# One group of transposes moved from TensorE to DMA, small loads to ScalarE's queue, and a rewritten order of work in a gated long-convolution and MLP kernel

## The chip, the core and the metric

The kernel runs on one core of a Trainium2 chip. A core has TensorE (PE in the profile; it multiplies, and it also transposes 128x128 blocks by multiplying with an identity), VectorE (DVE), ScalarE (ACT), GpSimd (POOL) and SyncE (SP, which here issues nearly all DMAs). ScalarE can issue DMAs too. TensorE writes only to PSUM, and VectorE or ScalarE must move each result from there to SBUF: such a move is called an evacuation below. The metric is the device time of one execution in microseconds (us).

## The reference

The inputs are q, k, v of 2048 tokens by 512 channels, a short kernel `shift_k` of 4 taps per channel, a long kernel `ssm_k` of 2048 taps per channel, a skip weight `ssm_D`, and an MLP of width 1376. The output is four residual layers on x = q:

```python
def _A_ref(q, k, v, shift_k, ssm_k, ssm_D):
    # k_shift[s] = sum over t of k[s - 3 + t] * shift_k[:, 3 - t]
    kv = k_shift * v
    y = irfft(rfft(pad(kv)) * rfft(pad(ssm_k)))[:S]      # causal convolution along the tokens
    y = y + kv * ssm_D
    return q * y
def _B_ref(x, w1, b1, w2, b2):
    y = _layernorm(x, axis=-1)
    return gelu(y @ w1 + b1) @ w2 + b2

x = A_q
x = x + _A_ref(_layernorm(x), A_k, A_v, A_shift_k, A_ssm_k, A_ssm_D)
x = x + _B_ref(_layernorm(x), B_w1, B_b1, B_w2, B_b2)
x = x + _A_ref(_layernorm(x), A_k, A_v, A_shift_k, A_ssm_k, A_ssm_D)
x = x + _B_ref(_layernorm(x), B_w1, B_b1, B_w2, B_b2)
```

The convolution does not depend on x, so it is computed once and its result y is used by both A layers.

## The kernel before, in words

The work has two parts. The first, up to about 100 us, computes y. The second runs the two MLP layers over the 16 token tiles in groups of four, eight rounds in all, each of two matrix products with the next group's normalisation beside them. The second part is not touched.

The first part consists of small pieces, each with a name. `plan.add` gives a piece its cost, what it depends on, and which buffer rings it takes from; `mm_evac` makes two pieces at once, a TensorE piece and its evacuation, whose name ends in `e`. The costs in the code are those that an offline planner used; at run time they have no effect. What the planner found is the long string `ORDER`: one word for each piece, such as `K26e.A` or `X01.20`. The letter after the dot is the engine (P TensorE, D VectorE, A ScalarE, G GpSimd, S SyncE); digits are buffer numbers, for a TensorE piece that of the PSUM buffer it fills. The kernel is written out in that order, so every engine runs its own pieces strictly in that order, and a piece that waits holds up all that stand behind it on its engine. There are four PSUM buffers `p` of 1024 float32 columns; a TensorE piece must wait until the one named for it is evacuated.

The pieces, in about the order of the data (cc counts four groups of 128 channels, j four groups of eight frequencies):

- loads: `lk0` to `lk3` (k), `lh1`, `lh113` (k, shifted rows), `lv0`, `lv1` (v), `lK00` to `lK11` (the long kernel, 128-byte runs), `lX`, `lW`, `lM` (transform tables), `lx0`, `lx1` (q, token groups 0 and 1), `lx` (all of q as the residual x), `lsT` and `lSK` (the short kernel, twice), `w1` to `w4` (MLP weights and output bias), `lb0`, `lb1` (the first MLP bias, loaded as single 2-byte elements).
- `kT`: transposes of k. `dg`: diagonal matrices of the short kernel. `kv`: the short convolution of channel groups 0 to 2 on TensorE, and `kvm` its product with v on VectorE. Group 3 has its short convolution on GpSimd: `kg0`, `kg1`, `ka1`, ..., `ka3`, then `kgm`, the product with v. Its two scratch tiles are T buffers 0 and 2, which the `T` pieces take later.
- `s00`, `s10`: layer-norm statistics of token groups 0 and 1, either on VectorE (batch-norm instructions) or on ScalarE (eight passes); `s01`, `s11`: what GpSimd adds to them; `s02`: the normalisation of group 0.
- `U`: the forward transform of kv, first stage (`U1S0` and so on), then a transposition: on TensorE (`U1T0`, `U1T1`, sixteen 128x128 blocks each, with an evacuation of 2048 columns) or by a DMA with transpose. `UT = "PPPX"` says which, one letter for each channel group: P TensorE, X DMA.
- `kd`, `KS`, `K2`: the transform of the long kernel; `sa0` to `sb3`: copies of it from SBUF to SBUF with its rows exchanged.
- `X` (second stage), `T` (product of the two spectra, on VectorE), `V` (first inverse stage), `Z` and `TC`, `TD` (transposition by DMA, and on TensorE), `Y` (last inverse stage), then gate, statistics and normalisation of the first tokens (`g0`, `h0`, `p0`, `b0`) and `LT0`, the transposition that the MLP starts from.

In the profile a helper's line stands for many pieces: L216 and L218 are evacuations on ScalarE and VectorE, L304 the U stage, L336 its transposes on TensorE, L382 KS, L395 K2, L506 kv, L512 kvm, L540 X, L555 T, L564 V, L599 TC and TD, L631 Y, L686 and L720 the MLP, L280 ordinary loads, L353 the lK loads, L283 transposes of U by DMA, L611 those of Z.

One more thing sets the order on the DMA queue. The framework counts the completion of DMAs on eight semaphores, DMAHW0 to DMAHW7, taken in turn in the order in which the program writes the DMAs, whichever engine issues them. From the ninth on, a DMA is issued only once the one eight places before it has landed.

Of the kernel before, what the change touches and what calls it, by code (L numbers as in the profile page):

```python
# [104 lines left out]
def kernel(ctx: ExitStack, tc: tile.TileContext, A_q, A_k, A_v, A_shift_k, A_ssm_k, A_ssm_D,  # L105
                 B_x, B_w1, B_b1, B_w2, B_b2, out):
    nc = tc.nc
    P = 128
# [76 lines left out]
    nc.scalar.dma_start(Ft[:], F_h.ap().bitcast(BF16))  # L185
    nc.scalar.dma_start(apf(arena, 40 * K, [[32 * ROW, 4], [1, D]]), apf(A_ssm_D, 0, [[0, 4], [1, D]]))
# [27 lines left out]
    def evac(eng, dst, src):  # L214
        if eng == "A":
            nc.scalar.activation(dst, src, AF.Copy)  # L216
        else:
            nc.vector.tensor_copy(dst, src)  # L218
# [590 lines left out]
```

## Time and profile before

| | us |
|---|---|
| time, median of 3 runs | 253.29 (253.15 to 253.44) |
| time of the profiled execution | 253.65 |
| its span, first to last instruction | 251.9 |
| first MLP product starts | 94.8 |
| busy in the span: TensorE, VectorE, ScalarE, GpSimd | 236.9, 169.7, 146.5, 54.6 |

All times inside the kernel are counted from the span's start. The profiled execution's own time is 1.75 us above its span. A row of the timeline gives start, duration, engine, line, operation, output<-input, shapes and a count of merged instructions; in brackets stands the engine's idle time before it and what ended it. Engine names with a q (SPq, ACTq) are the engine's queue of DMA issues: the duration of such a row is the time of issuing, not of the transfer.

### The profile page before, as it was taken

What the parts mean: (1) busy time and instruction counts of PE and PEld (TensorE: products, weight loads), DVE (VectorE), ACT (ScalarE), POOL (GpSimd) and SP (SyncE); (2) the same over time, 40 slices, a digit from 0 to 9 for tenths busy, and PEclk for the clock granted to TensorE, in tenths of its full rate; (3) what the DMA queues carried; (4) which work ended last, traced back from release to release, by engine and by line L of the source; (5) the groups of instructions that cost most, each with busy time, mean ns of one, the idle gap of its engine ahead of it and who ended that gap; (6) DMA issues with size and microseconds to landing.
All of it is one profiled execution on the core that took longest, in us unless ns stands there. A gap on an engine that the chain in (4) does not pass through costs nothing.

```text
span 251.9 us, 5135 instructions
## 1 busy us (share of the span) xinstructions
PE 236.9 (94%) x2104; PEld 146.1 (58%) x2104; DVE 169.7 (67%) x319; ACT 146.5 (58%) x212; POOL 54.6 (22%) x52
## 2 busy tenths in 40 slices
PE   2688999999999999999999999999999999999995
PEld 1588767899998738844444444444444444444443
DVE  0335889989999794987889899886866862022022
ACT  3598899999999798903803803803703712712810
POOL 3199999510000011011111101110110110000000
DMA  5999994698929993022040403107006006001001
GB/s 130 367 349 183 239 428 191 209 390 300 232 44 181 175 318 113 0 48 39 1 83 0 86 0 61 22 0 86 1 28 139 3 25 143 0 23 64 0 21 62
DMA packets 53040, 30.15 MB, mean 120 GB/s; under 512 B 46642, under 2 KB 50456, under 8 KB 51736
## 3 DMA queue, kind: packets, MB, share of 16 engines
q1 hardware_dynamic: 52864, 29.73, 45.0%
q8 instruction: 16, 0.26, 0.4%
q10 hardware_dynamic: 152, 0.09, 0.1%
q14 instruction: 8, 0.07, 0.1%
HBM read 16.71 MB, written 2.10 MB: 75 GB/s over the span
## 4 chain that ended last, share of the span: by engine, by line
PE 70%; DVE 9%; ACT 8%; DMA 8%; issue 4%; ACTq 0%; SPq 0%; DVEq 0%
PE po L720 30%; PE ph L686 29%; DVE arena L218 4%; DMA arena<-in_A_q_dram 3%; DMA arena<-in_B_w_dram 3%; DVE T L555 2%; PE p L506 2%; PE p L336 2%; ACT arena L216 2%; ACT ZT L216 2%; DVE ZT L218 2%; DMA arena<-in_A_ssm_D_dram 2%; ACT xb L216 2%; ACT arena L469 1%; PE p L382 1%
## 5 line engine op out<-in xcount | busy, mean ns | idle before, releaser
L688 ACT ACTIVATE arena<-ph,B 128x512 bf16<-128x512 f32 (+5 forms) x110 | 63.5, 609 | 81.9 <-PE ph L686 81.8
L686 PE MATMUL ph<-arena 128*128 128x512 bf16 (+4 forms) x440 | 78.5, 336 | 0.9 <-DMA arena<-in_B_w_dram 0.5
L720 PE MATMUL po<-arena 128*128 128x512 bf16 (+2 forms) x363 | 77.4, 372 | 0.0
L686 PEld LDWEIGHTS <-arena 128*128 128x128 bf16 (+1 forms) x440 | 40.5, 100 | 38.0 <-DMA arena<-in_B_w_dram 1.0
L720 PEld LDWEIGHTS <-arena 128*128 128x128 bf16 (+1 forms) x363 | 35.4, 98 | 40.5
L725 DVE TENSOR_TENSOR arena<-po,arena 128x512 bf16<-128x512 f32 (+1 forms) x33 | 21.5, 673 | 43.6 <-PE po L720 43.6
L216 ACT ACTIVATE arena<-p 128x1024 bf16<-128x1024 f32 (+6 forms) x40 | 38.8, 1040 | 7.9 <-PE p L423 4.5
L250 POOL TENSOR_TENSOR lrsm<-lrsm,mhalf 128x4 f32<-128x4 f32 (+2 forms) x10 | 8.9, 885 | 96.6 <-DVE lrsm L244 96.6
L216 ACT ACTIVATE ZT<-p 128x1024 bf16<-128x1024 f32 (+1 forms) x22 | 21.6, 1038 | 0.1
L238 DVE BATCH_NORM_STATS2 lstm<-arena 128x6 f32<-128x512 bf16 x32 | 19.9, 681 | 0.2
L218 DVE CAST arena<-p 128x1024 bf16<-128x1024 f32 x15 | 17.8, 1221 | 1.6 <-PE p L382 1.4
L555 DVE TENSOR_TENSOR T<-xb,arena 128x2048 bf16<-128x2048 bf16 (+1 forms) x17 | 18.8, 1163 | 0.0
L564 PE MATMUL p<-arena,T 128*128 128x128 bf16 x256 | 16.5, 219 | 1.1 <-DVE arena L218 0.4
L250 POOL TENSOR_TENSOR lrsg<-lrsg,mhalf 128x4 f32<-128x4 f32 x8 | 8.1, 1014 | 40.8 <-DVE lrsg L247 40.8
L437 POOL TENSOR_TENSOR T<-arena,SK 128x2048 bf16<-128x2048 bf16 (+3 forms) x4 | 15.0, 3751 | 5.1 <-DMA arena<-in_A_k_dram 5.0
L216 ACT ACTIVATE xb<-p 128x1024 bf16<-128x1024 f32 x15 | 15.9, 1132 | 0.1
L564 PEld LDWEIGHTS <-T 128*128 128x128 bf16 x256 | 14.9, 98 | 1.7 <-issue 1.4
L238 DVE BATCH_NORM_STATS2 lstg<-arena 128x6 f32<-128x512 bf16 x24 | 14.8, 680 | 0.0
L218 DVE COPY arena<-p 128x2048 bf16<-128x2048 bf16 (+3 forms) x10 | 10.4, 1049 | 5.9 <-issue 3.7
L255 DVE TENSOR_SCALAR arena<-arena,lmvg,lrsg 128x512 bf16<-128x512 bf16 x28 | 9.7, 408 | 6.7 <-POOL lrsg L250 6.7
L255 DVE TENSOR_SCALAR arena<-arena,lmvm,lrsm 128x512 bf16<-128x512 bf16 x32 | 11.2, 409 | 2.3 <-POOL lrsm L250 2.3
L506 PE MATMUL p<-DG,arena 128*128 128x128 bf16 x192 | 11.4, 219 | 1.3 <-ACT ZT L216 0.9
(78 smaller groups left out, 222.8 us busy)
## 6 DMA issues: line engine op xcount, KB each, us to landing
arena<-arena SPq DMA_DIRECT2D x8, 512.0 KB, 4.5
arena<-in_A_k_dram SPq DMA_DIRECT2D x4, 512.0 KB, 6.7
arena<-in_A_v_dram SPq DMA_DIRECT2D x2, 1024.0 KB, 10.8
arena<-in_A_ssm_k_dram SPq DMA_DIRECT2D x4, 512.0 KB, 7.1
arena<-tabM SPq DMA_DIRECT2D x1, 2048.0 KB, 12.5
arena<-in_A_q_dram SPq DMA_DIRECT2D x1, 2048.0 KB, 9.1
out_dram<-arena SPq DMA_DIRECT2D x15, 128.0 KB, 1.7
arena<-in_B_w_dram SPq DMA_DIRECT2D x1, 1376.0 KB, 7.8
```

The lines of the kernel that those rows point to most:

```text
L216: nc.scalar.activation(dst, src, AF.Copy)
L218: nc.vector.tensor_copy(dst, src)
L238: nc.vector.bn_stats(self.st[:, i, 0, :], x_t[:, GT * g + i, :] if src is None else src[:, i, :])
L250: nc.gpsimd.tensor_tensor(self.rs[:, a:b], self.rs[:, a:b], mhalf[:, a:b], ALU.pow)
L255: nc.vector.tensor_scalar(out=dst[:, i, :], in0=xs, scalar1=self.mv[:, i, 0:1], scalar2=self.rs[:, i:i + 1], op0=ALU.subtract, op1=ALU.mult)
L506: nc.tensor.matmul(o[:, i, :], w, DG[:, cc, t, :], start=t == 0, stop=t == KS - 1)
L555: eng.tensor_tensor(view(Tb[it["slot"]["T"]], [2, n, CW]), x2, kk, ALU.mult)
L564: nc.tensor.matmul(o[:, i, :], T[:, r, i, :], Mt[:, ka + i, 1 - r, :], start=r == 0, stop=r == 1)
L686: nc.tensor.matmul(o.rearrange("p (i t) -> p i t", t=P), W1t[:, ct, ft * P:ft * P + m], lt[:, a:b, ct, :], start=ct == 0, stop=ct == CT - 1)
L688: nc.scalar.activation(hT[0:m, ft, a * P:b * P], o, AF.Gelu_apprx_tanh, bias=B1[0:m, ft:ft + 1])
L720: nc.tensor.matmul(po[:, a:b], hT[0:m, ft, i * P:(i + 1) * P], W2t[0:m, ft, a:b], start=ft == 0, stop=ft == FT - 1)
L725: nc.vector.tensor_tensor(xs, po[:, a:b], xs, ALU.add)
```

## The change

Six edits:

1. `UT` becomes "PPXX": channel group 2 of the U stage is transposed by DMA as well, in place of two TensorE pieces and two evacuations.
2. The two loads of the short kernel (`lsT`, `lSK`) leave the plan and are issued by ScalarE, between the load of `Ft` and that of `ssm_D`.
3. The residual x is loaded in four pieces `lr0` to `lr3` instead of one `lx`; they depend on two more TensorE pieces, and three of them stand behind `w1` in the queue.
4. The MLP weights depend on fewer `T` pieces: `w1` on the first two of each channel group, `w2` to `w4` on the second and third.
5. The planner's costs of `KS`, `dg`, `kv`, `s00`, `s10` and `s02` are other numbers (at run time without effect), and `s02` may run on ScalarE alone.
6. `ORDER` is rewritten: other sequences on every engine, some pieces on another engine. Statistics `s00` go from ScalarE to VectorE and `s10` from VectorE to ScalarE.

The diff, without the rows of the table that only give the order:

```diff
 ORDER = """
-lSK.S lk1.S lsT.S lk3.S lk0.S lk2.S bSK.P3 lh1.S bSKe.A ...
+lk1.S lk0.S bSK.P2 lk2.S lk3.S bSKe.D lh113.S lh1.S lH.S lx1.S sF.G dg0.D dg1.A ...
 """
...
     nc.scalar.dma_start(Ft[:], F_h.ap().bitcast(BF16))
+    nc.scalar.dma_start(sT[:], A_shift_k.rearrange("(ct p) k -> p ct k", p=P))
+    nc.scalar.dma_start(SKr, apf(A_shift_k, (CT - 1) * P * KS, [[P * KS, 1], [1, P * KS]]))
     nc.scalar.dma_start(apf(arena, 40 * K, [[32 * ROW, 4], [1, D]]), apf(A_ssm_D, 0, [[0, 4], [1, D]]))
...
-    UT = "PPPX"
+    UT = "PPXX"
     ZM = "XXPP"
-    KSC, K2C = 440, 440
+    KSC, K2C = 560, 440
...
-        lS = [load("lsT", sT[:], A_shift_k.rearrange("(ct p) k -> p ct k", p=P), 2 ** 17),
-              load("lSK", SKr, apf(A_shift_k, CK * P * KS, [[P * KS, 1], [1, P * KS]]), 2 ** 13)]
+        lS = [None, None]
...
-            dg.append(plan.add(f"dg{ct}", {"D": 600, "A": 1000}, [sf], diag))
+            dg.append(plan.add(f"dg{ct}", {"D": 700, "A": 1250}, [sf], diag))
...
-            s0 = plan.add(f"s{n}0", {"D": 3190, "A": 4700}, [ld], stat)
+            s0 = plan.add(f"s{n}0", {"D": 3190, "A": 6500}, [ld], stat)
...
-            return s0, plan.add("s02", {"D": 1350, "A": 2200}, [s1], apply) if n == 0 else s1
+            return s0, plan.add("s02", {"A": 2900}, [s1], apply) if n == 0 else s1
...
-                pe = plan.add(f"kv{cc}{o2}", {"P": 1800}, kTe + [dg[cc]],
+                pe = plan.add(f"kv{cc}{o2}", {"P": 1880}, kTe + [dg[cc]],
...
-        lx = load("lx", x_t[:], q_d.rearrange(TOK, p=P), 2 ** 21, USp)
...
-        w1 = load("w1", W1t[:], B_w1.rearrange("(ct p) f -> p ct f", p=P), 1376 << 10, sum(Tcc, []))
-        wd = sum(Tcc, [])
-        w2 = load("w2", W2t[:, 0:FT - 1, :], B_w2[0:(FT - 1) * P, :].rearrange("(ft p) d -> p ft d", p=P), 1280 << 10, wd)
+        lx = [load(f"lr{g}", x_t[:, GT * g:GT * g + GT, :], xd[:, GT * g:GT * g + GT, :], 2 ** 19, USp + Xcc[3][:2],
+                   rank=2 if g else 0) for g in range(4)]
+        w1 = load("w1", W1t[:], B_w1.rearrange("(ct p) f -> p ct f", p=P), 1376 << 10, sum((t[0:2] for t in Tcc), []))
+        wd, we = sum(Tcc, []), sum((t[1:3] for t in Tcc), [])
+        w2 = load("w2", W2t[:, 0:FT - 1, :], B_w2[0:(FT - 1) * P, :].rearrange("(ft p) d -> p ft d", p=P), 1280 << 10, we)
...
-            ga = plan.add(f"g0{a}", {"D": 1190 if m == 2 else 930}, [y, s2, lx], gate, free=yf)
+            ga = plan.add(f"g0{a}", {"D": 1190 if m == 2 else 930}, [y, s2, lx[0]], gate, free=yf)
```

The order of the instructions is shown at three places. Line numbers of the changed kernel are higher by up to two (L280 becomes L282, L218 becomes L220).

First, SyncE's queue at the start of the program. `kh` is written by `lh1` and `lh113`, T1 by `lx1`, the 128x2048 load from `q` into the arena is `lx0`, those of 128x4096 are `lv0` and `lv1`, and those from `ssm_k` are `lK`. Before:

```order
L280 DMA arena_64<-in_A_shift_k_dram 1x512
L280 DMA arena_64<-in_A_k_dram 128x2048
L280 DMA sT_69<-in_A_shift_k_dram 128x4x4
L280 DMA arena_64<-in_A_k_dram 128x2048 x3
L280 DMA kh_68<-in_A_k_dram 112x3x128 [waits DMAHW0_49]
L280 DMA kh_68<-in_A_k_dram 15x3x128 [waits DMAHW1_49]
L280 DMA arena_64<-in_A_q_dram 128x2048 [waits DMAHW2_49]
L280 DMA arena_64<-in_A_v_dram 128x4096 [waits DMAHW3_49]
L280 DMA arena_64<-in_A_v_dram 128x4096 [waits DMAHW4_49]
L353 DMA arena_64<-in_A_ssm_k_dram 128x32x64 [waits DMAHW5_49]
```

and now:

```order
L282 DMA arena_64<-in_A_k_dram 128x2048 x4
L282 DMA kh_68<-in_A_k_dram 15x3x128 [waits DMAHW0_49]
L282 DMA kh_68<-in_A_k_dram 112x3x128 [waits DMAHW1_49]
L282 DMA GPt_75<-tabGP 128x256 [waits DMAHW2_49]
L282 DMA T1_104<-in_A_q_dram 128x2048 [waits DMAHW3_49]
L282 DMA arena_64<-in_A_q_dram 128x2048 [waits DMAHW4_49]
L282 DMA arena_64<-in_A_v_dram 128x4096 [waits DMAHW5_49]
L282 DMA arena_64<-in_A_v_dram 128x4096 [waits DMAHW6_49]
L355 DMA arena_64<-in_A_ssm_k_dram 128x32x64 [waits DMAHW7_49]
```

`lx1` (T1), which stood behind the tables, now stands ahead of `lx0`, v and the long kernel. ScalarE issues four DMAs ahead of these (DMAHW0 to 3) where it issued two, so that the loads of v now wait for the second and third load of k, and the first `lK` for the fourth.

Second, GpSimd at the end of group 3's short convolution. L444 (now L445) is `ka3`, L448 (L449) `kgm`, L523 (L524) `B1`, the cast of the MLP bias. Before:

```order
L437 TENSOR_TENSOR T2_103<-arena_64,SK_66 128x1664
L439 TENSOR_TENSOR T2_103<-kh_68,SK_66 128x384
L444 TENSOR_TENSOR T0_101<-T0_101,T2_103 128x2048
L448 TENSOR_TENSOR arena_64<-arena_64,T0_101 128x16x128
L523 CAST B1_77<-b1T_78 128x11
L250 TENSOR_TENSOR lrsg1_109<-lrsg1_109,mhalf_79 128x4
```

and now:

```order
L438 TENSOR_TENSOR T2_105<-arena_64,SK_66 128x1664
L440 TENSOR_TENSOR T2_105<-kh_68,SK_66 128x384
L445 TENSOR_TENSOR T0_103<-T0_103,T2_105 128x2048
L524 CAST B1_77<-b1T_78 128x11
L449 TENSOR_TENSOR arena_64<-arena_64,T0_103 128x16x128
L252 TENSOR_TENSOR lrsm0_114<-lrsm0_114,mhalf_79 128x1 x2
```

`B1`, which waits for the load `lb0`, now stands ahead of `kgm`; the power of the statistics of group 1 (`s11`) has gone to an earlier place on GpSimd, behind `s01`.

Third, VectorE at the end of K2. The 2048-column COPY rows are the evacuations of the U transposes, L555 is T. Before:

```order
L218 CAST arena_64<-p1_120 128x2x2x256
L238 BN_STATS lstg1_107<-T1_102 128x6 x4
L242 BN_AGGR lmvg1_108<-lstg1_107 128x2 x4
L247 TENSOR_SCALAR lrsg1_109<-lmvg1_108 128x4
L218 COPY arena_64<-p0_119 128x16x128
L218 COPY arena_64<-p2_121 128x16x128
L218 COPY arena_64<-p0_119 128x16x128
L218 CAST ZT2_97<-p2_121 128x256x4
L555 TENSOR_TENSOR T0_101<-xb0_98,arena_64 128x2048
L555 TENSOR_TENSOR T1_102<-xb1_99,arena_64 128x2048
```

and now:

```order
L220 CAST arena_64<-p2_123 128x2x2x256
L220 CAST arena_64<-p3_124 128x2x2x256
L220 COPY arena_64<-p2_123 128x16x128
L220 COPY arena_64<-p3_124 128x16x128
L555 TENSOR_TENSOR T0_103<-xb0_100,arena_64 128x2048
L220 COPY arena_64<-p1_122 128x16x128
L220 COPY arena_64<-p0_121 128x16x128
L555 TENSOR_TENSOR T1_104<-xb1_101,arena_64 128x2048
```

The statistics of group 1 are gone from here (they run on ScalarE ahead of the first U evacuations), and the first T stands between the copies of U0 and those of U1. Of the transposes of U2 one copy had stood on VectorE and one on ScalarE; both are gone.

6 lines of the change are left out of this document (3 added, 3 removed).

## The prediction

> **What bounds the kernel now.** I read the chain that ended last first: from 101 us on it is only L686 and L720, each group of 44 matmuls following the last. So the kernel has two parts, and I cut the span there and at the marks of the first part. Columns: stretch, length, then busy time of TensorE, its weight loads, VectorE, ScalarE, GpSimd, the clock, DMA share, GB/s.
>
> ```profile
> 13.40:41.00 27.60, 26.21 (x516) 21.41 (x514) 19.05 (x17) 25.07 (x40) 26.96 (x15) 1.00 1.05 303
> 41.00:82.40 41.40, 39.42 (x631) 36.57 (x631) 40.21 (x44) 41.10 (x45) 7.85 (x4) 1.00 0.78 211
> 82.40:94.80 12.40, 11.61 (x98) 7.04 (x96) 10.68 (x23) 10.29 (x12) 1.10 (x2) 1.00 1.05 249
> 101.40:251.90 150.50, 147.59 (x715) 70.52 (x715) 94.23 (x220) 57.88 (x90) 13.09 (x13) 1.00 0.19 39
> ```
>
> The last 150.5 us are TensorE's at full clock, and the change has nothing in them. What it can win is the start of the MLP, 94.8. Between 41.0 and 82.4 ScalarE is busy 41.10 of 41.40 us; between 13.4 and 41.0 it is busy 25.07 of 27.60 and VectorE only 19.05. TensorE reads full in both, but its rows stretch where it waits for PSUM. Its pieces alone, from the timeline:
>
> ```profile
> 13.22 3.75 PE L506 MATMUL p<-DG,arena 128*128 128x128 bf16 x64 [0.47 <-ACT arena L216]
> 27.23 0.27 PE L372 MATMUL p<-arena,IDt 128*128 128x64 bf16 x1
> 28.43 0.31 PE L377 MATMUL p<-Ft,IDt 128*128 128x320 bf16 x1
> ...
> 29.01 0.31 PE L377 MATMUL p<-Ft,IDt 128*128 128x320 bf16 x1
> ...
> 41.06 0.27 PE L395 MATMUL p<-arena,Wt 64*128 64x256 bf16 x1
> ...
> 44.96 0.36 PE L395 MATMUL p<-arena 64*128 64x256 bf16 x2
> 45.07 0.36 PE L395 MATMUL p<-arena,Wt 64*128 64x256 bf16 x2
> ...
> 50.75 2.26 PE L336 MATMUL p<-IDt,ZT 128*128 128x128 bf16 x32
> 52.85 0.60 PE L304 MATMUL p<-Ft,arena 128*128 128x256 bf16 x4
> 53.28 1.18 PE L336 MATMUL p<-IDt,ZT 128*128 128x128 bf16 x16
> ...
> 82.09 2.44 PE L599 MATMUL p<-IDt,ZT 128*128 128x128 bf16 x32 [0.37 <-DVE ZT L218]
> ```
>
> The reader is to take the distance from start to start where nothing waits: kv 1.86 each (3.75 for two), KS 0.58 (28.43 to 29.01), U stage 0.43 (52.85 to 53.28), a U transpose 1.05 (two from 50.75 to 52.85), a K2 of eight matmuls 0.45 (two every 0.11 us). But the sixteen K2 take from 41.06 to 50.75 with one transpose among them, 0.54 each: they go at the pace at which PSUM is emptied. Who empties it:
>
> ```profile
> 41.80 12.15 ACT L216 ACTIVATE arena<-p 128x1024 bf16<-128x1024 f32 x12
> 42.53 5.91 DVE L218 CAST arena<-p 128x1024 bf16<-128x1024 f32 x5
> ```
>
> Over the whole stretch 41.0 to 82.4 ScalarE makes 45 evacuations in 41.10 us, 0.92 each. One of the twelve here is a 2048-column copy of U2: 12.15 less 11 x 0.92 leaves 2.0 for it. VectorE's casts cost 1.15 from start to start (5.91 for five, their ends overlapping). So the first part is bound by evacuations, ScalarE's first, with VectorE (40.21 of 41.40) close behind it; what TensorE waits for is a free buffer.
>
> **The change part by part.** *Work moved.* Statistics on the two engines, and what goes with them:
>
> ```profile
> 13.43 0.63 ACT L469 ACTIVATE arena<-arena 128x512 bf16<-128x512 bf16 x1 [0.27 <-DMA arena<-in_A_q_dram]
> 19.86 0.18 ACT L472 ACTIVATION_READ_ACCUMULATOR arena<-arena,as 128x1 f32 x1
> 22.58 2.93 ACT L490 ACTIVATE arena<-arena,am,lrsg 128x512 bf16<-128x512 bf16 x4 [0.72 <-POOL am L482]
> 48.35 2.47 DVE L238 BATCH_NORM_STATS2 lstg<-T 128x6 f32<-128x512 bf16 x4
> 51.22 1.23 DVE L218 COPY arena<-p 128x2048 bf16<-128x2048 bf16 x1
> ```
>
> s10 leaves VectorE at 48.35 (to 51.22: 2.9) in its full stretch and becomes ScalarE's 6.6 us (13.43 to 20.04) early; s00 takes its 2.9 on VectorE early, where that idles 8.5 us. U2's transposes leave TensorE (2 x 1.05 = 2.1), VectorE (1.2) and ScalarE (2.0). Counted in ORDER, ScalarE makes 13 casts before K2 in place of 17 (4 x 0.95 = 3.8 less), and from K2 to the last V 42 and a half in place of 42 and a half with the U2 copy among them (2.0 - 0.9 = 1.1 less): 4.9 us less. VectorE has 18 evacuations and products and s00 before K2 (23.7 us) in place of 15, and 37.3 after K2 in place of 39.2.
>
> *By hand through the new order*, with these durations, every piece waiting for its engine, its buffer and its input. DMA first:
>
> ```profile
> 16.01 1.23 DVE L512 TENSOR_TENSOR arena<-p,arena 128x1024 bf16<-128x1024 f32 x1 [2.21 <-DMA arena<-in_A_v_dram]
> 18.67 2.36 DVE L512 TENSOR_TENSOR arena<-p,arena 128x1024 bf16<-128x1024 f32 x2 [1.43 <-DMA arena<-in_A_v_dram]
> 8.85 10.68 SPq L353 DMA_DIRECT2D arena<-in_A_ssm_k_dram  x2
> 59.68 9.04 SPq L283 DMA_TRANSPOSE arena<-ZT  x2
> ```
>
> lv0 and lv1 landed at 16.0 and 18.7. lx1's 512 KB ahead of them cost 1.3 (v's 1 MB took 2.7): 17.3 and 20.0. kT ends as before (13.1: dg1 and dg2 fill ScalarE's idle time before it). VectorE: s00 14.7 to 17.7, first product to 19.0, then from 20.0 products and U evacuations back to back, kv's last product to 28.1. ScalarE: s10 13.4 to 20.0. kd0 then falls at 26.5 (27.23 before), the first KS at 27.6. From 28.1 VectorE has ten casts (11.5, to 39.6), ScalarE ten and a short kd, and K2, which needs every KS evacuated and a buffer, starts at 38.8: 2.3 earlier, with three U stages put off behind it. From 39.3 ScalarE has 42.5 x 0.92 = 39.1 to do, and VectorE's 37.3 fit between: the last V is evacuated at 78.8, with waits of 0.4 in all, against 82.4: -3.6. The DMAs that now carry U2 (issue 2.0 each, or up to 7.0 behind a full queue, as the two of U3 took 9.04 together) are issued from about 50 on behind sb3, and X needs the first at 63: even 7.0 and the 3.7 that such a DMA takes to land fit.
>
> *The late part*, 82.4 to 94.8, has the same TensorE pieces; w1 was the last to come:
>
> ```profile
> 82.72 2.69 SPq L611 DMA_TRANSPOSE arena<-ZT  x2
> 85.50 2.41 SPq L280 DMA_DIRECT2D arena<-in_B_w_dram  x3
> 86.98 7.79 DMA arena<-in_B_w_dram
> 94.82 2.07 PE L686 MATMUL ph<-arena 128*128 128x128 bf16 x32 [0.52 <-DMA arena<-in_B_w_dram]
> ```
>
> Four Z stand between the last X (by the walk at 74) and w1: 4 x 1.35 (2.69 for two), so w1 is issued near 80 and lands within 9 us of it, some 2 us ahead of TensorE. Its wait of 0.52 goes; what is late next are the Y evacuations on ScalarE, 0.9 each against 0.86 of TensorE, so I count 0.2 of the 0.5. lr1 to lr3 and w2, 2.8 MB, follow w1: at the 249 GB/s of that stretch 11 us, from 85 to 96, and the first of them is read when group 1 is normalised, after 98 (101.4 less 3): hidden, with 2 us to spare.
>
> *Edits counted at nothing.* First the rows for the short kernel's loads and the last k:
>
> ```profile
> 0.80 0.35 SPq L280 DMA_DIRECT2D arena<-in_A_shift_k_dram  x1
> 1.64 0.42 SPq L280 DMA_DIRECT2D sT<-in_A_shift_k_dram  x1
> 11.89 0.85 PE L423 MATMUL p<-IDt,arena 128*128 128x128 bf16 x12 [0.28 <-DMA arena<-in_A_k_dram]
> ```
>
> The four-piece x takes 1.5 MB from behind the sa and sb copies to the late part; before, nothing waited for U3's transposes behind it. `w2` to `w4` freed early stand behind w1 in the queue anyway. s11 adds 0.9 to GpSimd's chain ahead of kgm, covered by the wait for lb0 (first rival). Issuing the shift loads on ScalarE frees SyncE of 0.35 and 0.42 and gives them to ScalarE, which has nothing else to do then; ssm_D is issued 0.8 later behind them, and with it GpSimd's sF and the dg, which the landing of k at 11.9 hides. The edit lies between -0.4 (the first k is issued at 0.8, not at 1.2, and all k lands that much earlier) and +0.8 (if dg came last); I take 0, since kv also needs the two kT evacuations that stand behind dg on ScalarE.
>
> The Trainium skill, "DMA: Bandwidth & Descriptors", section "Issuing engines are not separate DMA queues", says that DMAs issued on any engine run on the same 16 DMA engines, so that a second issuing engine saves only issue time. By it this edit would be worth the -0.4 at most and the sum -3.4; no run here yet shows it.
>
> The sum: -3.6 - 0.2, and +0.8 for waits between engines that a walk misses, of the kind that TensorE's waits show even now, when one engine alone is the bound:
>
> ```profile
> PE p L564 <- DVE arena L218: 0.4, 1, 0.4
> PE p L564 <- DVE ZT L218: 0.4, 1, 0.4
> ```
>
> Together -3.0. The profiled execution, 253.65 with span 251.9, gives 250.65; the median stands 0.36 lower: **250.3**.
>
> **The rivals.**
>
> *kgm late (gain of 0 to 2).* GpSimd's rows, VectorE's first T, and the time of lb0 from issue to landing:
>
> ```profile
> 39.49 4.06 POOL L444 TENSOR_TENSOR T<-T,T 128x2048 bf16<-128x2048 bf16 x1
> 43.63 4.06 POOL L448 TENSOR_TENSOR arena<-arena,T 128x2048 bf16<-128x2048 bf16 x1
> 50.43 0.19 POOL L523 CAST B<-b1T 128x11 f32<-128x11 bf16 x1 [2.74 <-DMA b1T<-in_B_b_dram]
> 56.92 2.35 DVE L555 TENSOR_TENSOR T<-xb,arena 128x2048 bf16<-128x2048 bf16 x2
> b1T<-in_B_b_dram SPq DMA_DIRECT2D x1, 2.5 KB, 4.2
> ```
>
> Before, kgm ended at 47.7 and no T came before 56.9; B1 came later. Now kgm waits for B1, B1 for lb0, lb0 stands behind sb1 and sb1 waits for the third K2 evacuation on ScalarE (42.1): lb0 issued 43.1, landed 47.3 by its 4.2, kgm to 51.5, just where my walk has the first T. Every us that lb0 takes more stalls VectorE's T, the U3 stage and the xb buffers. At 6 us in place of 4.2 the gain is 3.0 - 1.8 = 1.2 and the time 252.1. For it: the whole queue of sa and sb copies stands around this load. Against it: before, two of them stood ahead of lb0, now one.
>
> *TensorE was the bound after all*: 39.42 of 41.40 busy. Then only its 2.1 us of removed transposes count: 251.2. Against it: K2 at 0.54 where its matmuls need 0.45.
>
> *Slower: the long kernel comes late.* The first lK was issued at 8.85, when the first k pieces had landed; now it waits for the fourth, at 11.9 (kT's last wait). If its landing moves by that whole 3.05 and lx1's 1.3, the pair that kd0 needs, landed by 27.23 at the latest, comes at up to 31.6, 5.1 after my 26.5, and ScalarE idles: -3.0 + 5.1, 255.4. It decides from 29.5 on. Against it: the second lK's issue stood blocked for 9.42 us behind a full queue, so 3 MB of q and v still stand ahead of lK when it is issued at 11.9, and its landing should move by 1.3 only. From below, earlier landing gains nothing, as kd0 did not wait.
>
> *New order without effect*: by the counts above three engines now carry nearly the same from 13.4 to the last V (ScalarE and VectorE 62 and 61 us, TensorE about 61), so that each can stall the others; stalls of 3 us more than I took would bring 253.3.
>
> **How the numbers follow.** ScalarE relieved (248.8 to 251.5): 0.54. kgm late or TensorE bound (251.0 to 252.6): 0.22. No effect (252.3 to 254.3): 0.09, of which 0.05 within 0.2% of 253.29 (252.8 to 253.8; about what a measurement of this kernel can tell from no change) and 0.02 on either side. Long kernel late, or another stall of this size at the start (253.8 to 256): 0.15. The range, 248.8 to 253.2, reaches from the walk with the -0.4 and nothing for missed waits into the case of no effect, and leaves out 0.18 above and little below. Faster 0.54 + 0.22 + 0.02 = 0.78, same 0.05, slower 0.17.
>
> **What would show it.** Right: K2's first row (L396) near 39, the last V near 79, L688 starting near 91.5, ScalarE busy over 95% between; no wait of L688 for w1; VectorE's first T near 51.5. Wrong: GpSimd waiting for b1T beyond 48 with VectorE idle behind it; TensorE idle ahead of kd0 (L373) for ssm_k; VectorE idle for v beyond 1.5 us; L688 beginning later than 94.

## The result, and the profile after

The changed kernel takes 260.75 us (median of 4 executions, 260.69 to 261.31) against 253.37 us for the kernel before beside it (253.15 to 255.42): ratio 1.0278, 95% interval 1.0223 to 1.0333. It is slower, where 250.3 was forecast, and outside the range. The profiled execution took 260.74, its span 259.0, 7.1 more than before's 251.9.

Where the 7.1 us lie is seen from marks, the first four of them first rows of their kind in TensorE's timeline:

| | first kv | first K2 | first TC (L599/L601) | first MLP (L686/L688) | end of span |
|---|---|---|---|---|---|
| before | 13.22 | 41.06 | 82.09 | 94.82 | 251.9 |
| after | 20.63 | 49.72 | 90.39 | 101.72 | 259.0 |
| after minus before | +7.4 | +8.7 | +8.3 | +6.9 | +7.1 |

So the whole loss is there when the short convolution starts; 1.25 more goes before K2, and 1.8 is won back behind it. The start comes first. These are rows of the chain that ended last, before and then after (start, length, what):

```profile
1.18 4.02 DMA arena<-in_A_ssm_D_dram
```

```profile
2.43 6.93 DMA arena<-in_A_ssm_D_dram
11.28 3.99 issue
15.27 4.44 DVE DG L418 x3
19.71 0.88 DVE arena L220
20.63 6.83 PE p L507 x96
```

ssm_D, 4 KB, now takes 6.93 us in place of 4.02 and lands at 9.36 instead of 5.20. Behind it stand, on GpSimd, the zeroing and copies for Dz, then sF, then kg0 and kg1; on VectorE dg0, which needs sF. After, GpSimd's timeline, then VectorE's and TensorE's:

```profile
9.40 0.19 POOL L194 MEMSET arena<- 128x96 bf16 x1 [7.36 <-DMA arena<-in_A_ssm_D_dram]
9.52 1.42 POOL L196 COPY Dz<-arena 1x128 bf16<-1x128 bf16 x4
11.01 0.20 POOL L362 CAST sF<-sT 128x16 f32<-128x16 bf16 x1
11.21 7.90 POOL L438 TENSOR_TENSOR T<-arena,SK 128x2048 bf16<-128x2048 bf16 x2
```

```profile
11.24 8.47 DVE L418 TENSOR_SCALAR DG<-IDt,sF 128x128 bf16<-128x128 bf16 x4 [3.40 <-POOL sF L362]
19.63 1.81 DVE L220 COPY arena<-p 128x1536 bf16<-128x1536 bf16 x2
```

```profile
16.40 0.10 PEld L507 LDWEIGHTS <-arena 128*128 128x128 bf16 x1 [5.40 <-ACT arena L218]
20.63 6.83 PE L507 MATMUL p<-DG,arena 128*128 128x128 bf16 x96 [9.45 <-DVE arena L220]
```

The first weight load of kv waits for ScalarE's kT evacuations, which stand behind its own share of the diagonals (dg1, dg2), until 16.40; the first matmul then waits for VectorE's until 20.63. So of the 7.4 us at this mark about 3.2 come from the late sF by way of ScalarE (13.22 to 16.40), and 4.2 are what VectorE loses beyond that.

The four multiplications of dg0 take 8.47 us. Before, twelve of the same shape took 2.04:

```profile
7.07 2.04 DVE L417 TENSOR_SCALAR DG<-IDt,sF 128x128 bf16<-128x128 bf16 x12 [7.07 <-POOL sF L361]
```

What differs is what GpSimd does beside them. Before, its timeline shows it waiting for k until 12.02, when the multiplications were done:

```profile
12.02 7.95 POOL L437 TENSOR_TENSOR T<-arena,SK 128x2048 bf16<-128x2048 bf16 x2 [4.98 <-DMA arena<-in_A_k_dram]
```

Now kg0 and kg1 run from 11.21 to 19.1, beside them. The view of line L418 gives the duration of one operation, minimum, median and maximum in ns:

```profile
L418 DVE TENSOR_SCALAR DG<-IDt,sF x4: 241/2178/4112, 11.2 to 19.5; 128x128 bf16<-128x128 bf16 x4
```

The longest, 4112 ns, is as long as one kg0 or kg1 (7.90 for two). Windows of 0.04 us show the edges: the first operation runs from 11.24 to 15.4, where kg0 ends (15.3), the second to 19.2, where kg1 ends (19.1), and the other two fill the last 0.6. Behind dg0 stand the two kT evacuations on VectorE, and behind those kv: TensorE idles 9.45 us.

The clock is the second loss. Windows of the changed kernel (stretch, length, busy time of TensorE, its weight loads, VectorE, ScalarE, GpSimd, then the granted clock, DMA share, GB/s):

```profile
13.60:23.30 9.70, 2.67 (x26) 2.78 (x27) 9.70 (x10) 8.99 (x20) 5.89 (x3) 0.50 1.05 337
43.90:50.90 7.00, 7.00 (x90) 4.48 (x91) 3.51 (x4) 4.10 (x5) 4.62 (x2) 0.51 0.02 4
49.72:90.90 41.18, 39.44 (x613) 35.54 (x612) 38.78 (x35) 39.89 (x45) 4.27 (x2) 0.99 0.92 200
90.90:101.80 10.90, 10.90 (x98) 7.11 (x97) 9.67 (x20) 9.47 (x12) 1.51 (x2) 1.00 1.05 312
109.00:259.00 150.00, 146.89 (x711) 69.88 (x708) 93.50 (x218) 57.58 (x88) 13.10 (x13) 1.00 0.18 39
```

The clock is granted at half from 13.6 to 23.3, where TensorE stood still for most of the time, and again for 7 us about the start of K2 (49.72), where it is busy. Before, it was 1.00 in every stretch. The third row is the evacuation-bound stretch, with ScalarE busy 39.89 of 41.18 as it was 41.10 of 41.40; the fourth is the late part, in which TensorE no longer idles; the last is the MLP, unchanged.

For the numbers below: executions of one and the same kernel, before included, differ by 1.5 to 5 us with the mean clock granted (1.00, 0.993, 0.987, 0.98), and the ratios leave out those more than 1.5% above the fastest of their kernel, while the medians are of all.

### The profile page after: what moved, and what is told of

Same layout as the page of the kernel before. It is cut to its first block, busy times and chain, and to the rows that moved or that the text cites. A ratio compares the mean times of both kernels' runs of the same rounds, so it can differ in the third digit from the quotient of the medians.

```text
span 259.0 us, 5078 instructions
## 1 busy us (share of the span) xinstructions
PE 237.0 (91%) x2072; PEld 146.2 (56%) x2072; DVE 179.9 (69%) x315; ACT 142.7 (55%) x214; POOL 55.1 (21%) x52
## 4 chain that ended last, share of the span: by engine, by line
PE 78%; DVE 8%; ACT 4%; issue 4%; DMA 3%; ACTq 1%; POOL 1%; DVEq 0%; POOLq 0%
PE po L722 29%; PE ph L688 28%; PE p L507 5%; ACT arena L218 4%; DVE T L555 4%; DMA arena<-in_A_ssm_D_dram 3%; PE p L306 3%; PE p L564 2%; PE p L383 2%; DVE DG L418 2%; PE p L396 2%; PE p L338 2%; PE p L378 2%; DVE arena L220 1%; PE p L540 1%
## 5 line engine op out<-in xcount | busy, mean ns | idle before, releaser
L688 PE MATMUL ph<-arena 128*128 128x512 bf16 (+4 forms) x440 | 78.5, 336 | 0.4 <-ACT arena L218 0.2
L688 PEld LDWEIGHTS <-arena 128*128 128x128 bf16 (+1 forms) x440 | 40.5, 100 | 37.2 <-issue 0.4
L218 ACT ACTIVATE arena<-p 128x1024 bf16<-128x1024 f32 (+6 forms) x38 | 34.9, 984 | 5.8 <-PE p L383 2.0
L218 ACT ACTIVATE ZT<-p 128x1024 bf16<-128x1024 f32 (+1 forms) x19 | 19.4, 1081 | 7.6 <-PE p L306 7.5
L507 PE MATMUL p<-DG,arena 128*128 128x128 bf16 x192 | 12.7, 231 | 9.4 <-DVE arena L220 9.4
L220 DVE CAST arena<-p 128x1024 bf16<-128x1024 f32 x15 | 17.9, 1220 | 2.2 <-PE p L383 1.4
L555 DVE TENSOR_TENSOR T<-xb,arena 128x2048 bf16<-128x2048 bf16 (+1 forms) x17 | 18.7, 1154 | 0.3 <-ACT xb L218 0.3
L507 PEld LDWEIGHTS <-arena 128*128 128x128 bf16 x192 | 12.4, 104 | 9.6 <-ACT arena L218 5.4
L240 DVE BATCH_NORM_STATS2 lstg<-arena 128x6 f32<-128x512 bf16 x28 | 17.2, 676 | 0.0
L218 ACT ACTIVATE xb<-p 128x1024 bf16<-128x1024 f32 x15 | 15.8, 1119 | 0.0
L220 DVE CAST ZT<-p 128x1024 bf16<-128x1024 f32 (+1 forms) x10 | 11.5, 1163 | 2.1 <-ACT arena L218 1.6
```

The source lines that it names most:

```text
L240: nc.vector.bn_stats(self.st[:, i, 0, :], x_t[:, GT * g + i, :] if src is None else src[:, i, :])
L507: nc.tensor.matmul(o[:, i, :], w, DG[:, cc, t, :], start=t == 0, stop=t == KS - 1)
L555: eng.tensor_tensor(view(Tb[it["slot"]["T"]], [2, n, CW]), x2, kk, ALU.mult)
L688: nc.tensor.matmul(o.rearrange("p (i t) -> p i t", t=P), W1t[:, ct, ft * P:ft * P + m], lt[:, a:b, ct, :], start=ct == 0, stop=ct == CT - 1)
```

## The experiments

The theory after the two traces: the two loads on ScalarE's queue are the whole loss. Their 4 KB and 1 KB consist of very small pieces, which take turns with k's large packets on the same DMA engines and hold up ssm_D behind them; sF comes too late for dg0 to get ahead of kg0; and while GpSimd runs kg0, VectorE's dg0 is shut out. The rivals: the new order, not the loads, makes the loss; dg0 is slow by itself or for want of data.

| run | first kv | first K2 | first MLP | time, median (range, executions) |
|---|---|---|---|---|
| before with the loads on ScalarE | 19.93 | 49.14 | 102.60 | 261.44 (1) |
| after with the loads on SyncE | 12.23 | 41.13 | 93.06 | 252.3 (250.1 to 255.69, 10) |
| after, ssm_D ahead of them | 20.14 | 47.28 | 99.05 | 258.1 (1) |
| after, kg0 behind dg0 | 14.70 | 43.63 | 95.25 | 255.16 (253.28 to 257.18, 10) |
| after, dg0 on ScalarE | 15.85 | 46.11 | 98.44 | 257.46 (1) |

**The one edit alone, in the kernel before.** `lsT` and `lSK` leave the order; nothing else changes.

```diff
+    nc.scalar.dma_start(sT[:], A_shift_k.rearrange("(ct p) k -> p ct k", p=P))
+    nc.scalar.dma_start(SKr, apf(A_shift_k, (CT - 1) * P * KS, [[P * KS, 1], [1, P * KS]]))
...
-        lS = [load("lsT", ...), load("lSK", ...)]
+        lS = [None, None]
```

> The kernel before, with only the two loads of the short kernel moved to ScalarE's queue (all else, the order too, as before). 'Lock': sF is ready near 11, kg0 starts at once or soon behind it, and the twelve diagonal products on VectorE are held back by kg0 and kg1: first kv at 20 or later, 259 to 262. If only the late input counts: dg 11 to 13, first kv near 15, 254.5 to 256.

It took 261.44 against 253.13 for before: +8.3 from this edit alone, more than the whole change. GpSimd's and VectorE's timelines:

```profile
10.68 7.95 POOL L438 TENSOR_TENSOR T<-arena,SK 128x2048 bf16<-128x2048 bf16 x2
```

```profile
10.61 9.75 DVE L418 TENSOR_SCALAR DG<-IDt,sF 128x128 bf16<-128x128 bf16 x12 [10.61 <-POOL sF L362]
```

The same picture as in the changed kernel, twelve multiplications of 2.04 us in 9.75.

**The change without this edit.**

```diff
-    nc.scalar.dma_start(sT[:], ...)
-    nc.scalar.dma_start(SKr, ...)
+    nc.sync.dma_start(sT[:], ...)
+    nc.sync.dma_start(SKr, ...)
```

> The changed kernel, with the two loads of the short kernel issued by SyncE (first in its queue) instead of ScalarE. 'Lock, set off by the late loads': sF is ready near 7 and dg0 is done before kg0 starts near 10 to 12; first kv near 12.5 to 13; if TensorE's clock then stays whole, 250 to 251.5; if the second fall of the clock (44 to 51 us) remains, 252 to 253.5. Rival 'the new order itself is worse': 255 or more, though dg0 is quick.

252.3 us against 253.13 for before, ratio 0.9944 (0.9894 to 0.9994), and 250.1 and 250.36 in the two executions at full clock, where before's fourteen full-clock ones in the same comparison lie between 252.17 and 253.70. dg0 is 0.74 us again, long before kg0:

```profile
5.18 0.74 DVE L418 TENSOR_SCALAR DG<-IDt,sF 128x128 bf16<-128x128 bf16 x4 [0.91 <-POOL sF L362]
```

So the other five edits together gain about 2.7 us at full clock and 0.8 by the medians, and the one moved pair of loads costs about 8. The new order as such is not the loss.

**Which load is late, and why.** The table of DMA issues gives the time from issue to landing of the 4 KB of sT: before, after, and with the loads on SyncE ahead of k:

```profile
sT<-in_A_shift_k_dram SPq DMA_DIRECT2D x1, 4.0 KB, 4.5
```

```profile
sT<-in_A_shift_k_dram ACTq DMA_DIRECT2D x1, 4.0 KB, 8.4
q10 hardware_dynamic: 682, 0.09, 0.3%
```

```profile
sT<-in_A_shift_k_dram SPq DMA_DIRECT2D x1, 4.0 KB, 2.1
q10 hardware_dynamic: 152, 0.09, 0.1%
```

q10 is ScalarE's queue. The two loads add 530 packets to it, for 5 KB. To tell waiting behind them from their own slowness, ssm_D was issued ahead of them:

```diff
+    nc.scalar.dma_start(apf(arena, 40 * K, [[32 * ROW, 4], [1, D]]), ...)
     nc.scalar.dma_start(sT[:], ...)
     nc.scalar.dma_start(SKr, ...)
-    nc.scalar.dma_start(apf(arena, 40 * K, [[32 * ROW, 4], [1, D]]), ...)
```

> The changed kernel with the load of ssm_D ahead of the two loads of the short kernel on ScalarE's queue. Theory A (the 512 pieces of 8 bytes of the short kernel wait between the large packets of k, and ssm_D waited behind them): ssm_D lands near 5 as before, GpSimd has zeroed and copied Dz by 6.5 and waits only for sT; sF comes at 8.5 to 9.5, dg0 gets in ahead of kg0 at 10.8 in about 0.75 us, first kv near 13.5 to 14.5, time 253 to 255. Theory B (only the issue times count: 0.8 us): ssm_D lands at 5, sF by 6.5, first kv at 12.2 as in e2_shift_on_sync, 252.3. If sF still comes after 10.7: locked as in the changed kernel, 260.

```profile
6.18 0.19 POOL L194 MEMSET arena<- 128x96 bf16 x1 [4.13 <-DMA arena<-in_A_ssm_D_dram]
6.30 1.40 POOL L196 COPY Dz<-arena 1x128 bf16<-1x128 bf16 x4
10.48 0.20 POOL L362 CAST sF<-sT 128x16 f32<-128x16 bf16 x1 [2.78 <-DMA sT<-in_A_shift_k_dram]
10.71 7.91 POOL L438 TENSOR_TENSOR T<-arena,SK 128x2048 bf16<-128x2048 bf16 x2
```

ssm_D is early again, but sT itself lands only at 10.4, and dg0 takes 8.51 us, as it took 8.47 in the changed kernel. So ssm_D had waited behind the two loads, sT is slow by itself beside k, and neither of the two places tried on ScalarE's queue helps: my window of 8.5 to 9.5 for sF was a microsecond too hopeful, and with it the 253 to 255. The Trainium skill, "DMA: Bandwidth & Descriptors", section "Queues, rings and completion order", says that each DMA engine goes round between the queues that have work, a packet at a time. The 8.4 us beside k and 2.1 ahead of it on one queue agree with many tiny packets that each wait for a large one of the other queue; the taking of turns itself is in no view here.

**Is it kg0 that shuts dg0 out?** First GpSimd is held back: it reads four numbers of dg0's result before kg0 starts.

```diff
+                nc.gpsimd.tensor_copy(dgr[:], DG[:, 0, :, 0])
```

> The changed kernel, with one GpSimd copy of four elements of the first diagonal matrix ahead of kg0, so that kg0 starts only when VectorE's dg0 is done; nothing else moves. Theory 'lock' (VectorE's dg0 cannot run while GpSimd's kg0 and kg1 run): dg0 takes about 1 us instead of 8.5, the first kv starts near 16.3 (when ScalarE has done dg1, dg2 and two kT evacuations) instead of 20.6, time 256 to 257. Rival 'late input' (only the late arrival of ssm_D and sF counts, and dg0 is slow for a reason of its own, such as the DMA traffic): dg0 still takes about 8 us, time 260 to 262.

dg0 then takes 0.74 us and the time is 255.16 against 253.13 for before, ratio 1.0059 (1.0007 to 1.011):

```profile
9.53 0.74 DVE L419 TENSOR_SCALAR DG<-IDt,sF 128x128 bf16<-128x128 bf16 x4 [1.84 <-POOL sF L363]
```

sF came at 9.30 in this profile, not at 11.01, so part of the gain is not the wait's, and first kv comes at 14.70, ahead of the 16.3 expected. The time stays 2.9 above the 252.3 with the loads on SyncE: the late input costs something without the lock too. Second, dg0 is given to ScalarE, behind dg1 and dg2, with kg0 left where it was:

```diff
-... sF.G dg0.D dg1.A kT1.P3 lx0.S dg2.A ...
+... sF.G dg1.A kT1.P3 lx0.S dg2.A dg0.A ...
```

> The changed kernel, with dg0 on ScalarE behind dg1 and dg2, so that no diagonal is made on VectorE; loads as late as in the changed kernel. 'Lock': the kT evacuations on VectorE come at 11 to 13, those on ScalarE at 14.9 to 17.6, first kv near 17.7, time near 257.5. 'Late input' alone: as the changed kernel, 260 to 261.

```profile
9.51 3.61 ACT L416 ACTIVATE DG<-IDt,sF 128x128 bf16<-128x128 bf16 x12 [4.94 <-POOL sF L362]
```

Twelve in 3.61 us, 0.30 each, with kg0 running beside most of them: ScalarE is not shut out, VectorE is. The time of the one execution, 257.46, is better than the changed kernel's 260.75, though ScalarE's kT evacuations now start 3.75 behind sF, where they started 2.58 behind it; here too sF came early, at 9.28.

The cleanest case is a second victim, which I had not expected. With the loads back on SyncE, VectorE's last operation of s00, four numbers in each partition, takes 2.23 us, to the end of kg1, and its first product and TensorE wait:

```profile
16.48 2.23 DVE L249 TENSOR_SCALAR lrsg<-lmvg 128x4 f32<-128x4 f32 x1
18.63 4.93 DVE L513 TENSOR_TENSOR arena<-p,arena 128x1024 bf16<-128x1024 f32 x4
```

```profile
19.90 0.61 PE L306 MATMUL p<-Ft,arena 128*128 128x256 bf16 x4 [2.14 <-DVE arena L513]
```

The view of its line has seven such operations in the kernel, at a median of 0.17 us (minimum, median, maximum in ns):

```profile
L249 DVE TENSOR_SCALAR lrsg<-lmvg x7: 169/170/2232, 16.5 to 193.6; 128x4 f32<-128x4 f32 x7
```

That operation alone was moved to GpSimd:

```diff
                 if it["eng"] == "D":
                     S.part(n, 0, GT, x)
-                    S.join(0, GT)
+                    for i in range(GT):
+                        nc.vector.bn_aggr(S.mv[:, i, :], S.st[:, i, 0:1, :])
...
+                else:
+                    nc.gpsimd.tensor_scalar(out=S.rs[:], in0=S.mv[:, :, 1], scalar1=EPS, scalar2=None, op0=ALU.add)
                 S.scale(0, GT)
```

> The short kernel's loads on SyncE, and the last operation of s00 (128x4, adding epsilon) issued by GpSimd ahead of the power in place of VectorE. Theory A (VectorE's small tensor_scalar of 2.23 us stood locked out until GpSimd's kg1 ended at 18.6): VectorE's first product starts when v lands, near 16.5 to 17.3, TensorE's wait of 2.14 ahead of U1S0 falls to under 1, and kd0 starts 1 to 1.5 us before 27.0; the time falls by about as much, to 251 where the clock stays as it was. Rival (it waited for v and the lock only covered that): the first product stays at 18.6 with a wait for v in its bracket, and the time stays at 252.3.

```profile
16.53 1.19 DVE L516 TENSOR_TENSOR arena<-p,arena 128x1024 bf16<-128x1024 f32 x1
19.35 1.23 DVE L516 TENSOR_TENSOR arena<-p,arena 128x1024 bf16<-128x1024 f32 x1 [1.63 <-DMA arena<-in_A_v_dram]
```

The first product starts at 16.53 while kg1 still runs; the second waits for v, and kd0 comes at 25.76 instead of 27.02. The time is 251.64 (248.85 to 252.43, 4) against 253.64 for before, ratio 0.9894 (0.9826 to 0.9961); in the one execution at full clock 248.85 against 250.1. VectorE's statistics (four in 2.47 us), its PSUM copies (0.96) and its products from PSUM (1.19) take beside GpSimd what they take without it; its operations with a scalar and all their data in SBUF do not. The Trainium skill, "SBUF — State Buffer", section "Who interferes with whom", states such a rule: VectorE in a two-port mode and GpSimd take one port pair, whoever is first has it for the whole instruction, and the other is fully blocked. The 4112 ns beside a GpSimd instruction of 4 us agree.

**kgm, and the half clock.** The prediction's rival "kgm late" was tried on the last kernel:

```diff
-... U0T0.P2 B1.G kgm.G ...
+... U0T0.P2 kgm.G B1.G ...
```

> The kernel of e7_s00_tail_on_gpsimd with kgm ahead of B1 on GpSimd, and nothing else. If kgm's place behind B1 held up the first T (the prediction's rival kgm late): kgm ends near 48 in place of 54.1, the first T starts 1 us or more before 55.1 and the last V and L688 with it, 250 to 250.5 at the clock that e7 had in its median. If not: kgm ends near 48, the first T stays at 55 since it waits for an X evacuation, and the time is that of e7, 248.9 at full clock and 251 to 252.5 where a half-speed stretch is in it.

kgm ends at 48.06 in place of 54.06, and the first T starts at 54.59 in place of 55.15, while K2 itself began 0.96 earlier in this profile:

```profile
44.00 4.06 POOL L449 TENSOR_TENSOR arena<-arena,T 128x2048 bf16<-128x2048 bf16 x1
```

```profile
54.59 1.23 DVE L558 TENSOR_TENSOR T<-xb,arena 128x2048 bf16<-128x2048 bf16 x1 [0.33 <-ACT xb L218]
```

T waits for X's evacuation, not for kgm. This kernel takes 251.11 us (248.38 to 251.62, 6) against 253.12 for before, ratio 0.9877 (0.9821 to 0.9933): it beats both kernels, before by 1.2% by the ratio and 0.8% by the medians.

Its time goes with the half clock: 248.38 and 248.94 at 0.998, the other four 250.96 to 251.62 at 0.992 or 0.993. In the profile of the change with the loads on SyncE the clock stood at half from 38.4 to 41.9, with TensorE busy throughout (columns as in the windows above, two of the windows of 1 us):

```profile
36.00:37.00 1.00, 0.57 (x16) 0.37 (x17) 0.57 (x1) 0.17 (x1) 1.00 (x1) 1.00 1.14 483
39.00:40.00 1.00, 1.00 (x7) 0.69 (x6) 0.40 (x1) 0.93 (x2) 0.92 (x2) 0.50 1.11 475
```

Ahead of it stands a gap in which TensorE waits for nothing that the profile shows, in KS (L383):

```profile
35.48 0.23 PE L383 MATMUL p<-Ft,arena 32*128 32x64 bf16 x3
36.43 0.36 PE L383 MATMUL p<-Ft,arena 32*128 32x64 bf16 x13 [0.73 <-issue]
...
38.46 2.74 PE L306 MATMUL p<-Ft,arena 128*128 128x256 bf16 x12
```

I tried two cures. First, spreading the three U stages of channel group 0 among the KS pieces, as before had them, which also changes the buffers and the engines of some evacuations behind them:

```diff
-... KS70.P3 KS41e.A U0S0.P22 KS70e.A U0S0e.D U0S3.P0 U0S2.P1 U0S3e.A kg3.G K26.P3
+... KS21.P2 lW.S kg2.G KS01e.A lM.S U0S0.P32
...
+... KS20.P0 KS10e.D kd4e.A U0S3.P3
...
+... KS51.P1 KS50e.A U0S2.P2
```

> The short kernel's loads on SyncE as in the run e2_shift_on_sync, and in addition the three U stages of channel group 0 moved in between the KS pieces, as the order of before has them, in place of one block behind them. Theory A (TensorE's clock falls because sixteen KS pieces, mostly 32x64 matmuls, stand together without a larger product between them): no second dip, granted clock 1.00 from 28 to 50 us in the profile and 0.999 or more of the span in nearly all runs, K2 starting 1 to 1.5 us earlier (40), median 250.3 to 251. Theory B (the dip is set off by the gap of 0.4 to 1.3 us in which TensorE waits for nothing that the profile shows, ahead of its 478th matmul): the gap stays at that count, whatever stands around it, and the dip follows it, clock 0.98 to 0.993, median 252 to 253. Theory C (the dips belong to the chip and not to the order): the same, without a gap.

The profile has full clock throughout, and the gap all the same, 0.72, so a gap need not bring the half clock; but 8 of the 10 executions have 0.993 or less, as without it, and K2 now waits 1.50 for an evacuation. The time is 254.72 (252.04 to 256.38, 10) against 253.64 for before, ratio 1.0003 (0.9957 to 1.0048). Theory A, that KS pieces standing together make the loss, falls. This order, the operation of s00 on GpSimd and kgm first together did no better:

> The short kernel's loads on SyncE, the U stages of group 0 among the KS, the last operation of s00 on GpSimd, and kgm ahead of B1 on GpSimd. If the lock and the clock were all that kept the change from its gain: granted clock 0.999, kgm ending at 47 in place of 53.9, the first T near 51.5, K2 starting near 39.5, median 249 to 250, ratio to before 0.984 to 0.988. If the walk of the prediction was itself too hopeful between K2 and the last V: kgm early but the first T still above 53, and the median at 250.5 or more. If GpSimd's earlier kgm takes SBUF time from VectorE's products or collides with them: VectorE's T longer than 1.23 us each and no gain.

254.9 (251.57 to 256.64, 12) against 253.64, ratio 0.9954 (0.9899 to 1.0009), where 249 to 250 was expected; K2 waits 1.50 here too, so this order of U0 is worse than the changed kernel's. kgm ends at 47.97, and the first T still starts only at 56.26.

Second, the gap's place was moved by adding matmuls early, cutting bSK, into eight and then into 64:

```diff
-lambda o: nc.tensor.matmul(o, one[:], SKr, ...)
+lambda o: [nc.tensor.matmul(o[:, 64 * c:64 * c + 64], one[:], SKr[:, 64 * c:64 * c + 64], ...) for c in range(8)]
```

> The kernel of e7_s00_tail_on_gpsimd with the one 512-column product bSK cut into eight of 64 columns: seven more matmuls on TensorE at 3 us, where it idles. If the gap ahead of the 478th matmul belongs to a count of TensorE's instructions: it stays at the 478th, which is now seven matmuls earlier in the work (the 14th of KS41's sixteen small ones, not the 4th of KS70's), length 0.4 to 1.3. If it belongs to the place in the work: it stays ahead of KS70's 4th, now the 485th. If it goes away with the count and the clock loss has come from it: 0.999 or more in most runs, and a median near 249. If the clock loss is independent of it: again in 7 or 8 runs of 10 below 0.995, median 251 to 252.

> The kernel of e7_s00_tail_on_gpsimd with bSK cut into 64 matmuls of 8 columns: 63 more than in e7, all at 3 to 6.6 us where TensorE waits for k. The gap belongs to the count (e11_bsk_in_eight), so the 478th matmul falls 63 earlier in the work, three to four KS pieces, near 32 us. Theory A (the gap starts the half-speed stretch because the thinly filled KS work stands on both sides of it): a gap at 31 to 32.5 us still, the half-speed stretch moves with it to about 33 to 36 or goes, and the granted clock is 0.998 or more in more than half of the runs, median 249 to 250. Theory B (the half-speed stretch is not the gap's doing): it stays at 37 to 42 us, the granted clock stays under 0.995 in most runs, median 251 to 252.6.

252.61 (249.01 to 253.98, 10) against 253.12 for before and 251.55 (250.07 to 254.64, 10) against 253.42, ratios 0.9899 (0.9838 to 0.9959) and 0.9907 (0.9864 to 0.9951); 9 and 7 of the ten executions have a clock below 0.995. Windows that end inside the gap count the matmuls and weight loads ahead of it, here for eight and then for 64:

```profile
0.00:35.50 35.50, 26.62 (x477) 22.59 (x478) 22.07 (x29) 25.52 (x44) 27.12 (x32) 1.00 0.96 269
```

```profile
0.00:37.50 37.50, 30.96 (x605) 25.85 (x606) 24.29 (x31) 27.84 (x47) 28.94 (x32) 1.00 0.99 287
```

In all ten other profiles of the new order the gap stands behind the 477th matmul and the 478th weight load, with seven more matmuls too; with 63 more it has gone on to the 605th and 606th, that is 256 instructions later (955 to 1211), and nothing stalls at 955. So it goes by TensorE's instruction count, with one step of 256 seen, and not by the work. Which step stalls, and how long (0.19 to 1.29 us), and why before has no such gap, stays open. The 64 pieces did not bring the gap to 32 us, as was meant, but to 37.2, so that they do not settle whether it starts the half clock. That too stays open: in the four comparisons the granted clock was below 0.995 in 24 of 72 executions of before and in 47 of 62 of the seven kernels of the new order with the loads on SyncE. The new order loses it more often; the KS block does not account for it, and the gap is not shown to.

## Why the prediction was wrong

**The step that failed** is the edit counted at nothing: "Issuing the shift loads on ScalarE frees SyncE ... ssm_D is issued 0.8 later behind them, and with it GpSimd's sF and the dg, which the landing of k at 11.9 hides", between -0.4 and +0.8. It cost about 8. The issue was counted at 0.8 (1.25 in the trace, 1.18 to 2.43); what running beside k's 2 MB does to 512 pieces of 8 bytes was not: ssm_D 6.93 in place of 4.02 and sT 8.4 in place of 4.5. And the cover was wrongly drawn. k's landing hid a late dg only as long as dg came before kg0: before, GpSimd's kg0 waited for k until 12.02 and dg was done by 9.1; with sF at 11.01 kg0 follows it at once and starts together with dg0, and VectorE loses. I asked only how late dg would come, not what it would run beside. The rule of the Trainium skill that the prediction weighed, "DMA: Bandwidth & Descriptors", section "Issuing engines are not separate DMA queues", gave the loss no room either: by it the edit was worth 0.4 at most, and it cost about 8.

**The clock**, which the whole sum took as full, is the second thing missed: half for 9.7 us at the start and for 7 us about the start of K2. The first begins 2.4 us into TensorE's idle time. All five profiles with the loads on ScalarE, where TensorE idles 3.69 to 9.45 us ahead of kv, have such a stretch there, and none of the others has; that the idle time causes it was not tested by itself.

**The walk** can be judged on the run with the loads on SyncE. First kv 12.23 (walk 13.1), kd0 27.02 (26.5), K2 41.13 (38.8), L688 93.06 (91.5). Up to K2 it was 2.3 too hopeful: 0.5 up to kd0, where s00's locked operation stands (2.14 of TensorE's idle time), and 1.8 behind it, where the gap (0.73) and the half clock (twelve U matmuls in 2.74 against 1.48 before, 1.3) stand. None of them is in the walk.

**K2 to the last V**: a gain of 1.3 was forecast. From the first K2 to the first TC it is 41.03 before, 40.67 in the changed kernel and 40.56 with the loads on SyncE (41.13 to 81.69): 0.4 to 0.5. ScalarE is still the busiest evacuator, so the bound was rightly read; about a third of the term came.

**The late part** was mis-sized the other way: -0.2 forecast, -1.4 measured (first TC to first MLP, 12.73 before and 11.33 after). w1's wait went, as said; but TensorE's 11.61 busy before held rows stretched by waits too, and now the same 98 matmuls stand in 10.90 without idle time. The Y evacuations on ScalarE, 9.47 of 10.90 busy, did not come last.

**The rivals.** kgm late: B1 kept kgm until 62.70, 13.0 behind the first K2, where the walk had 12.7; lb0 took 2.9 us to land and not more than 4.2, as this rival needs, and the run with kgm first shows that T waits for X anyway. TensorE as the bound: K2 to the first TC would have fallen by the 2.1 of removed transposes, and fell by 0.4 to 0.5. Long kernel late: kd0 waits for nothing in any of these profiles. It had the right sign and a chance of 0.15 with "another stall of this size at the start", but 255.4 for the wrong wait, and 260.75 lies above every band that had a chance. The sum of the other edits, -3.0 forecast, was about -2.7 at full clock, but by other terms than mine (in that profile nothing up to K2, -0.5 from there to the first TC, -1.4 in the late part), so that the agreement is in part luck; the chance for faster, 0.78, hung on the edit I had put at nothing.

**What showed it**, by my own list: L688 later than 94 (101.72). GpSimd waited for b1T until 58.43, but VectorE did not idle for kgm, TensorE did not wait for ssm_k, and L688 does not wait for w1.

## What to carry to other kernels

Before a small load is moved to another engine's queue, ask what large load will be in flight beside it: a few hundred tiny pieces beside megabytes took 8.4 us, ahead of them on the same queue 2.1. When an early VectorE operation is to "hide" under a wait, list what GpSimd will run at that moment; here an operation with a scalar, all in SBUF, beside a long GpSimd operation took as long as what was left of that operation, even for four numbers, while statistics and moves out of PSUM took nothing extra. And an edit counted at nothing deserves the question what else its cover was waiting for.

## What the hardware showed that was not expected

A VectorE operation of 0.17 to 0.25 us took 2.23 and 4.11 us beside GpSimd. TensorE stalls for up to 1.29 us with nothing in the profile to wait for, at instruction counts 256 apart. The Trainium skill, "Runtime: NRT & Kernel Launch", section "Instruction fetch mechanics", says that instructions are fetched in blocks of 256 and that this is mostly hidden. The step agrees, and the stall here is not hidden; that it is such a fetch is not shown. And a clock of half was granted for 3.4 us (loads on SyncE) and 7 us (the changed kernel) while TensorE was busy throughout; of the ten executions of the kernel with the loads on SyncE two have full clock.
